# Attention, then a gated mixing layer, on one core: five blocks instead of three multiplied late by seven-product block multiplication, and the order of all work redrawn

## The chip, the cores and the metric

The kernel runs on one core of one Trainium2 chip. The metric is the time of one execution on the device, in microseconds (us); lower is better. The kernel before took 575.64 us (median of 3 runs, 574.69 to 575.94).

## What is computed

Cut to what matters, in float32 from end to end:

```python
scores = q @ k.T / sqrt(64) - log(448)          # 8 batches x 12 heads, 448 tokens, 64 wide
x = sigmoid(scores) @ v                         # put together: 8 x 448 x 768
gate = sigmoid(causal conv of x, 5 taps, per channel)
out = (gate * (x @ w_val)) @ w_out              # two 768 x 768 products
```

The engines that multiply fast take float16 or a rounded float32, so the kernel reaches float32 accuracy in one of two ways: it multiplies plain float32 tiles, which TensorE does in more passes, or it splits each operand into a high and a low part and adds three products (high x high, low x high, high x low).

## The kernel before, in words

**Units.** Two heads of one batch are a *pair* (48 of them, `st[i]`), two pairs a *two* (24, `two[j]`), and three twos fill one batch, called a *block* here (0 to 7). The tokens of block 0 are dealt out over blocks 1 to 7, so that the second stage has seven blocks of 512 tokens each.

**Attention.** `scores` (L581) multiplies a pair's keys and queries, chunk by chunk of 128 keys: three instructions of the plan per pair, each into one of three `ps_a` tiles of PSUM. Pairs in `WHOLE_SCORES` (0 to 14) use plain float32 (`qk_single`), the others `qk_hi` and `qk_lo`. The keys beyond three chunks come two pairs at a time from `scores_rest` (L616). `attention` (L655) takes a finished PSUM tile: ScalarE does the sigmoid (L659). For twos in `WHOLE` (0 to 8) that writes the float32 tile `a_single` and frees the bank. For the others the sigmoid stays in PSUM, ScalarE copies it out as float16 (L669, recorded as L404), VectorE subtracts to get the low part (L670), and only then is the bank free. `attend` (L693) multiplies by the values: a rest (L709) and four groups of chunks (L717). `out_of_ps` (L742) copies the result into `x`.

**Range of x.** A block with no two in `WHOLE` is `bounded`: the float16 scale of its x is taken from its values' largest, known early (`x_bound`, L602). In any other block VectorE has to find the largest x itself (L769), ScalarE spreads it on a diagonal (L809) and TensorE sends it to all partitions (`spread`, L811 to L813); `x_split` (L834) can come only after that.

**Second stage.** `product` (L849, its matmuls are L864) multiplies a block by `w_val` (named V below: 6 x 6 steps of three 512-column matmuls). The gate comes from five taps, on ScalarE, VectorE, GpSimd and by adding transfers. `y` is gate times product; blocks 1 to 4 go through `w_out` in the same way at once (O below, 6 x 6 x 3 = 108 matmuls of 512 columns), with y rounded by a transfer of GpSimd (L898) and its low part by VectorE or GpSimd (L899).

**Late blocks.** Blocks in `LATE` (5, 6, 7) store y to DRAM instead (L891), and are multiplied at the end by a scheme with seven half-size products in place of eight (`late_product`, L933; the matmuls are L956: 7 products x 3 parts x 3 x 3 = 189 matmuls of 256 columns per block). Its inputs, `out_forms` (L915), are sums and differences of quarters of y: loads through one buffer `y4` (L912), sums (L923), casts on ScalarE (L928, L929; recorded as L398), low parts (L930, L931; recorded as L409). Its outputs are scaled (L964), added (L973) and stored (L1001). The forms of successive late blocks live by turns in the tiles of the queries and keys and in the tiles of the attention weights, and so wait for those.

**Order.** Nothing is issued in the order of the code. Every step is an `op` with a cost per engine that may do it, a priority worked out from the table `AT`, and dependencies through its tiles; `Plan.issue` (L210) plays this through once, on the host, and writes each engine's instructions down in the order in which they start there. On the chip each engine then works through its own queue in that order. An op that two engines may do goes to the one that the plan finds free; `AT["share"]` (L249) says when VectorE may take a copy of ScalarE's. VectorE and GpSimd ops named `port="VG"` are kept from overlapping, on the chip by a dependency that is added at L1141.

Of the kernel before, what the change touches and what calls it, by code (L numbers as in the profile page):

```python
# [39 lines left out]
WHOLE = {*range(0, 9)}  # L40
WHOLE_SCORES = {*range(0, 15)}
# [40 lines left out]
LATE = (5, 6, 7)  # L82
AHEAD_OF_VAL = 3

FIRST_TOP = 6
SUMS = 12
OWN_BANKS = (6, 7)
# [5 lines left out]
BY_GPSIMD = ()  # L93
# [7 lines left out]
    first=-15.92, step=186.61, val=336.87, val_step=-29.39, out=-1237.15, out_step=257.57, w_max=1518.34,  # L101
    w_split=-860.95, load_qk_first=-201.47, load_qk=-1852.52, load_v=-662.01, split_hi=32.92, split_lo=-1097.78,
    rest_first=3174.29, rest=-1385.28, a_first=-2081.72, a=-74.73, attend=1686.54, v_max=-553.4, v_exp=-1453.48,
    v_split=144.91, x=-3266.86, x_max=-92.19, x_scale=515.03, x_hi=744.75, x_lo=177.24, x_step=2637.25,
    x_early=1120.5, first_max=-2492.59, tap=891.8, scores=8.56, a_rest=-659.37, a_rest_first=766.83,
    tap_first=-340.19, tap_pair=-743.04, tap_step=-330.6, gate=2823.26, product=-1112.74, y=2077.31, g_hi=-1119.86,
    g_lo=-3664.76, o=-3117.03, sums=-1119.35, f=-1154.59, late=-18.26, late_step=909.44, late_load=-912.54,
    pair0=2133.67, pair1=-1429.33, pair2=330.9, pair3=-1211.45, pair4=1377.13, pair5=-3156.16, pair6=297.98,
    pair7=-522.61, pair8=1609.62, pair9=-2397.11, pair10=-676.08, pair11=-98.56, pair12=-2966.57, pair13=-1287.04,
    pair14=1751.28, pair15=-717.37, pair16=545.19, pair17=-2818.83, pair18=-2085.26, pair19=495.26, pair20=75.11,  # L110
    pair21=-2539.24, pair22=-2144.55, pair23=158.2, val0=-2466.55, val1=1919.24, val2=208.28, val3=1536.8,
    val4=-2488.28, val5=-691.86, out0=173.81, out1=2060.89, out2=3408.9, out3=430.48, out4=2535.97, out5=-302.79,
    val_of1=-468.82, val_of2=-2362.91, val_of3=-1477.84, val_of4=1531.79, val_of5=1921.35, val_of6=-402.85,
    val_of7=1707.7, out_of1=-472.42, out_of2=247.7, out_of3=-1251.83, out_of4=-193.95, out_of5=1473.61,
    out_of6=-476.29, out_of7=-1672.61, share=2436.46, w_load=2736.66,
# [39 lines left out]
class Op:  # L155
    __slots__ = ("ways", "prio", "emit", "deps", "n", "start", "end", "eng", "after", "size", "port", "then")

    def __init__(self, n, ways, prio, emit, size, port):
        self.n, self.ways, self.prio, self.emit, self.size, self.port = n, ways, round(prio, 5), emit, size, port
        self.deps, self.after, self.then = set(), None, None  # L160
        self.start = self.end = self.eng = None


class Plan:
# [9 lines left out]
    YIELD = 0.3  # L174
    DMA_RATE = 310e3
# [5 lines left out]
    def op(self, ways, prio, emit, reads=(), writes=(), size=0, port="VG"):  # L181


        o = Op(len(self.ops), ways, prio, emit, size, port)
# [25 lines left out]
    def issue(self):  # L210
# [13 lines left out]
        events, order, bus, port = [], [], 0.0, 0.0  # L224
# [10 lines left out]
        while events:  # L235
# [6 lines left out]
            for e in engines:  # L242
                if free[e] > t:
                    continue
                for _, n in ready[e]:
# [3 lines left out]
                    if e == "V" and "A" in o.ways and free["A"] < t + AT["share"]:  # L249
                        continue  # L250
# [11 lines left out]
                cost = o.ways[e]  # L262
                o.eng, o.start = e, t
# [932 lines left out]
```

## Time and profile before

| what | before |
|---|---|
| median of 3 runs | 575.64 us |
| profiled execution | 575.5 us, of which the span from first to last instruction is 573.6 |
| TensorE (PE) busy | 563.7 us, 98% of the span |
| VectorE (DVE) | 423.6 us, 74% |
| ScalarE (ACT) | 401.6 us, 70% |
| GpSimd (POOL) | 242.6 us, 42% |
| granted TensorE clock | 0.998 of full speed |

A matmul's busy time reaches past the start of the next one, so "busy" does not tell how tightly TensorE is packed; the distance from one start to the next does. Weight loads are PEld and run beside the matmuls.

### The profile page before, as it was taken

The page shows a single profiled execution, that of the slowest core. Times are in us where ns is not written, and L with a number is a line of the kernel's source. Part 1 is how long each engine was busy: PE and PEld are TensorE (multiplying, and loading weights), DVE is VectorE, ACT ScalarE, POOL GpSimd, SP SyncE. Part 2 cuts the span into 40 slices and gives each one's busy share as a digit, 9 for nine tenths or more (in the row PEclk, how much of TensorE's full clock was granted, in tenths as well). Part 3 has the DMA queues.
Part 4 walks back from the last instruction along what each step waited for, and adds up shares of the span by engine and source line. Part 5 has one row for each costly group of instructions (what it writes and reads, how often), then busy time and mean ns, then how long its engine had stood idle before and what let it go on. Part 6 is the DMA issues. An engine that isn't in the chain of part 4 may idle for free.

```text
span 573.6 us, 9982 instructions
## 1 busy us (share of the span) xinstructions
PE 563.7 (98%) x3793; PEld 300.6 (52%) x3793; DVE 423.6 (74%) x653; ACT 401.6 (70%) x488; POOL 242.6 (42%) x301
## 2 busy tenths in 40 slices
PE   9999989999999999999999999999999999999996
PEld 4343334454554545545455445455555446865785
DVE  0867998896789775486766778866878999847544
ACT  5788986556987859677686878997889994332221
POOL 0001346866656285365734455545665421400100
PEclk9999999999999999999999999999999999999999
DMA  8987789968586979686495775976787565730122
GB/s 312 360 272 247 223 216 229 218 159 230 186 207 201 300 162 246 161 198 155 109 231 146 205 172 152 219 191 184 204 237 197 137 166 143 188 94 14 61 75 74
DMA packets 48400, 107.25 MB, mean 187 GB/s; under 512 B 15712, under 2 KB 24544, under 8 KB 48352
## 3 DMA queue, kind: packets, MB, share of 16 engines
q1 hardware_dynamic: 33808, 67.19, 34.3%
q0 software_dynamic: 14256, 39.23, 33.6%
q8 instruction: 30, 0.49, 0.3%
q10 hardware_dynamic: 288, 0.20, 0.1%
q14 instruction: 18, 0.15, 0.1%
HBM read 63.52 MB, written 17.90 MB: 142 GB/s over the span
## 4 chain that ended last, share of the span: by engine, by line
PE 89%; ACT 4%; DVE 3%; issue 2%; DMA 1%; POOL 1%; DVEq 0%; ACTq 0%
PE ps_m L864 42%; PE ps_a L592 15%; PE ps_a L717 15%; PE late L956 7%; PE ps_m L956 4%; PE ps_a L636 4%; PE ps_a L709 3%; ACT a_single L659 1%; DMA g<-y 1%; DVE a L670 1%; ACT gate L404 1%; PE ps_m L1023 1%; DVE gate L790 0%; POOL w_form L409 0%; DVE y L896 0%
## 5 line engine op out<-in xcount | busy, mean ns | idle before, releaser
L864 PE MATMUL ps_m<-xs,w_val_hi 128*128 128x512 f16 x504 | 150.1, 379 | 0.6 <-DVE y L896 0.6
L670 DVE SCALAR_TENSOR_TENSOR a<-ps_a,a 128x896 f16<-128x896 f32 x90 | 95.1, 1090 | 29.2 <-ACT a L404 29.0
L659 ACT ACTIVATE ps_a<-ps_a 128x896 f32<-128x896 f32 x105 | 93.2, 911 | 26.6 <-DVE v_exp L649 16.1
L864 PE MATMUL ps_m<-xs,w_val_lo 128*128 128x512 f16 x252 | 95.5, 379 | 0.0
L787 POOL TENSOR_SCALAR tap<-x,cw 128x512 f32<-128x512 f32 x84 | 69.2, 845 | 56.6 <-DVE gate L790 14.1
L409 POOL TENSOR_TENSOR qk_lo<-qk_src,qk_hi 128x448 fp32r<-128x448 f32 x66 | 74.9, 1156 | 29.9 <-DVE gate L790 11.1
L864 PE MATMUL ps_m<-g,w_out_hi 128*128 128x512 f16 x288 | 86.0, 380 | 0.5 <-POOL g L409 0.5
L404 ACT ACTIVATE a<-ps_a 128x896 f16<-128x896 f32 x90 | 80.1, 928 | 0.2
L864 PEld LDWEIGHTS <-w_val_hi 128*128 128x128 f16 x504 | 47.6, 98 | 60.0 <-issue 7.8
L790 DVE SCALAR_TENSOR_TENSOR gate<-x,cw,gate 128x512 f32<-128x512 f32 x84 | 65.3, 798 | 0.5 <-ACT gate L404 0.3
L659 ACT ACTIVATE a_single<-ps_a 128x896 f32<-128x896 f32 x63 | 53.6, 928 | 17.0 <-DVE out_inverse L434 8.5
L794 POOL DMA_DIRECT2D gate<-tap x42 | 38.8, 925 | 50.3 <-DMA gate<-tap 25.4
L864 PE MATMUL ps_m<-g,w_out_lo 128*128 128x512 f16 x144 | 54.6, 379 | 0.0
L717 PE MATMUL ps_a<-a,v_hi 128*64 128x448 f16 x360 | 49.4, 355 | 0.0
L864 PEld LDWEIGHTS <-w_out_hi 128*128 128x128 f16 x288 | 27.0, 98 | 35.0 <-issue 4.3
L717 PE MATMUL ps_a<-a_single,v_src 128*64 128x448 f32 x216 | 42.6, 543 | 0.0
L567 POOL DMA_DIRECT2D qk_hi<-qk x33 | 20.8, 630 | 48.4 <-PE ps_a L592 35.8
L592 PE MATMUL ps_a<-qk_hi 64*128 64x448 f32 x198 | 40.1, 401 | 0.8 <-DVE a_rest L670 0.8
L864 PEld LDWEIGHTS <-w_val_lo 128*128 128x128 f16 x252 | 24.7, 98 | 29.7
L592 PE MATMUL ps_a<-qk_single 64*128 64x448 f32 x180 | 37.2, 553 | 0.2 <-ACT a_single L659 0.2
L592 PE MATMUL ps_a<-qk_lo,qk_hi 64*128 64x448 f32 x198 | 36.3, 362 | 0.0
L592 PE MATMUL ps_a<-qk_hi,qk_lo 64*128 64x448 f32 x198 | 36.3, 362 | 0.0
(144 smaller groups left out, 936.4 us busy)
## 6 DMA issues: line engine op xcount, KB each, us to landing
gate<-tap POOLq DMA_DIRECT2D x42, 512.0 KB, 5.8
qk_src<-qk SPq DMA_DIRECT2D x33, 448.0 KB, 5.0
qk_hi<-qk POOLq DMA_DIRECT2D x33, 416.0 KB, 4.3
v_src<-vs SPq DMA_DIRECT2D x24, 448.0 KB, 4.1
qk_single<-qk SPq DMA_DIRECT2D x14, 448.0 KB, 6.2
out_t<-y SPq DMA_DIRECT2D x24, 224.0 KB, 2.1
w_words<-w_val SPq DMA_DIRECT2D x6, 768.0 KB, 7.9
w_words<-w_out SPq DMA_DIRECT2D x6, 768.0 KB, 4.8
```

Of the source, the lines that this page charges most:

```text
L404: nc.scalar.activation(to, x, AF.Copy, scale=by)
L409: engines[eng].tensor_tensor(to, x, y, op=ALU.subtract)
L592: mm(b()[:, h, :S], k()[rows, at : at + P], q()[rows, :S], start=(n == 0), stop=(n == len(terms(i)) - 1))
L636: mm(b()[to, h, :S], x[n]()[rows, CW:], x[n]()[rows, :S], start=True, stop=True)
L659: nc.scalar.activation(to, b()[:, :, :S], AF.Sigmoid, bias=-math.log(S), scale=1.0 / math.sqrt(D))
L670: op({"V": 1.0}, t + 0.5, lambda e: nc.vector.scalar_tensor_tensor(part(1), p(), A_SCALE, part(0), op0=ALU.mult, op1=ALU.subtract), [b], [ ...
L717: mm(px()[to, p, :S], v()[:, o : o + D], x(st[2 * j + p]["a", c])[:, h, at : at + S], start=(j == 0 and c == 0 and n == 0), stop=(j > 0 an ...
L787: op({"G": TAP_G}, at + AT["tap_step"] * k - AT["tap_first"] + AT["tap_pair"] * p, lambda e, p=p, k=k, tap=tap: nc.gpsimd.tensor_scalar(by ...
L790: op({"V": 0.67}, at + AT["tap_step"] * k + AT["tap_pair"] * p, lambda e, p=p, part=part, k=k: nc.vector.scalar_tensor_tensor(part(), x()[ ...
L794: op({"G": 1.1}, at + AT["tap_step"] * k, lambda e, tap=tap: nc.gpsimd.dma_start(g(), tap(), accum_op=ALU.add), [tap], [g], 4 * P * T * 4, "")
L864: mm(po()[:, cs], w()[:, c, :], x(k)[:, cs], start=(c == 0 and j == 0), stop=(c == NC - 1 and j == 2))
L956: mm(po()[:, i * HT : (i + 1) * HT], weights(w, k, c), gv[b, c][g]()[:, x, :], start=(c == 0 and i == 0 and j == 0), stop=(c == UNITS - 1 ...
```

## The change

It moves blocks 3 and 4 from the direct second product to the late scheme. Twos 13, 22 and 23 get plain float32 attention weights and values, pairs 15, 16 and 17 plain float32 scores. Block 4 and block 7 thereby stop being bounded and measure their largest x. A copy that ScalarE did alone, because the rule of `share` never let VectorE have it, is now given to VectorE where `ON_VECTOR` names it. Three low parts of weights are offered to GpSimd. The plan also counts a cost when TensorE goes from one shape of tile to another, and all numbers of `AT` are new. Cut to its core:

```diff
-WHOLE = {*range(0, 9)}
-WHOLE_SCORES = {*range(0, 15)}
+WHOLE = {*range(0, 9), 13, 22, 23}
+WHOLE_SCORES = {*range(0, 18)}
-LATE = (5, 6, 7)
+LATE = (3, 4, 5, 6, 7)
+FIRST_OUT = min({*range(1, B)} - {*LATE}, default=B - 2)
-OWN_BANKS = (6, 7)
-BY_GPSIMD = ()
+BY_GPSIMD = (("out", 4), ("out", 5), ("val", 1),)
+ON_VECTOR = {
+    "a": {13, 14, *range(27, 30), 38},
+    "forms": {18, 19, 31, 41},
+    "gate": {3},
+    "o": {*range(24, 27), 39, 45},
+    "parts": {27, 35},
+    "xs": {8},
+}
 AT = dict(
-    first=-15.92, step=186.61, val=336.87, val_step=-29.39, out=-1237.15, out_step=257.57, w_max=1518.34,
+    first=1148.39, step=658.12, val=11982.37, val_step=633.23, out=-10068.43, out_step=-8973.56, w_max=14984.15,
...
+    LEAVE = {"full": 0.0, "wide": 0.095, "tall": 0.098, "small": 0.0}
+    ENTER = {"full": 0.008, "wide": 0.1, "tall": 0.03, "small": 0.0}
...
-                    if e == "V" and "A" in o.ways and free["A"] < t + AT["share"]:
-                        continue
...
+                if e == "P":
+                    if o.form != form:
+                        cost += self.LEAVE[form] + self.ENTER[o.form]
+                    form = o.form
...
-    x_exp = ring(sb, 3, [P, 4], I32, "x_exp")
-    o_scale = ring(sb, 3, [P, NC], F32, "o_scale")
+    x_exp = ring(sb, 8, [P, 4], I32, "x_exp")
+    o_scale = ring(sb, 8, [P, NC], F32, "o_scale")
...
+    def way(kind, n, scalar, vector):
+        return {"V": vector} if n in ON_VECTOR.get(kind, ()) else {"A": scalar}
...
-        op({"A": 0.82, "V": 1.0}, t + 0.4, lambda e: scaled(e, part(0), p(), A_SCALE), [b], [a], port="")
+        op(way(tag, n, 0.82, 1.0), t + 0.4, lambda e: scaled(e, part(0), p(), A_SCALE), [b], [a], port="")
...
-            po = ps_a.new(lambda: ps.tile([P, 512], F32, name="late", tag="ps_a", bufs=ps_a.n)) if b in OWN_BANKS else ps_m.new()
+            po = ps_a.new(lambda: ps.tile([P, 512], F32, name="late", tag="ps_a", bufs=ps_a.n)) if b != LATE[0] else ps_m.new()
...
-            elif o.eng == "V" and o.ways["V"] > 0.2:
+            elif o.eng == "V":
                 last = traced
```

Lines of the changed file stand some 20 further down: its L404 is L424, L659 is L679, L409 is L429, L398 is L418, L567 is L587, L765 is L785, L787 is L807, L794 is L814, L796 is L816, L898 is L918.

The order at three places. First GpSimd's queue where block 2 is made ready for its product by `w_out` (O2), just ahead of the tokens' low parts. Before:

```order
L898 DMA g<-y 128x512
L898 DMA g_2043<-y 128x512
L794 DMA gate<-tap 128x1024
L567 DMA qk_hi<-qk 128x832
L765 MEMSET x 128x2x4
L409 TENSOR_TENSOR qk_lo<-qk_src,qk_hi 128x448
L409 TENSOR_TENSOR g<-y,g 128x512
L409 TENSOR_TENSOR g_2043<-y,g_2043 128x512
L409 TENSOR_TENSOR qk_lo<-qk_src,qk_hi 128x384
```

Now:

```order
L918 DMA g<-y 128x512
L918 DMA g_2078<-y 128x512
L429 TENSOR_TENSOR qk_lo<-qk_src,qk_hi 128x384
L785 MEMSET x 128x2x4
L814 DMA gate<-tap 128x1024
L587 DMA qk_hi<-qk 128x832
L807 TENSOR_SCALAR tap<-x,cw 128x512
L814 DMA gate<-tap 128x1024
```

The two low parts of y (g) have left GpSimd's queue; VectorE makes them. On TensorE, scores of pair 23 alone stood between the last product by `w_val` of block 2 and O2; now the remaining keys and values of two 11 and the scores of pair 24 do.

Second, ScalarE's queue around the last three pairs, 45 to 47 (the tile `a_rest` is the rest of two 23). Before:

```order
L404 ACTIVATE a<-ps_a 128x2x448
L404 ACTIVATE gate<-x,cw 128x512
L398 CAST forms<-y_4511 128x768
L398 CAST forms<-f 128x1024
L659 ACTIVATE ps_a<-ps_a 128x2x448
L404 ACTIVATE gate<-x,cw 128x512
L404 ACTIVATE a_rest<-ps_a 128x2x448
L404 ACTIVATE x<-ps_a,v_exp 128x2x7x64
L659 ACTIVATE ps_a<-ps_a 128x2x448
L796 ACTIVATE gate<-gate 128x1024
L404 ACTIVATE a<-ps_a 128x2x448
```

Now:

```order
L679 ACTIVATE a_single<-ps_a 128x896 x3
L418 CAST forms<-y_2873 128x768
L418 CAST forms<-f 128x1024
L679 ACTIVATE a_single<-ps_a 128x896
L418 COPY x<-ps_a 128x2x7x64
L679 ACTIVATE a_single<-ps_a 128x896 x3
L816 ACTIVATE gate<-gate 128x1024
L679 ACTIVATE a_single<-ps_a 128x896 x3
```

Each PSUM tile of these pairs now takes one instruction of ScalarE and none of VectorE.

Third, ScalarE's queue from the last copy of x (two 23) on, which has a new step. Before:

```order
L404 ACTIVATE x<-ps_a,v_exp 128x2x7x64
L398 CAST forms<-f 128x1024
L404 ACTIVATE gate<-x,cw 128x512
L404 ACTIVATE xs<-x,x_exp 128x1024
L404 ACTIVATE gate<-x,cw 128x512
```

Now:

```order
L418 COPY x<-ps_a 128x2x7x64
L418 CAST forms<-f 128x1024
L424 ACTIVATE gate<-x,cw 128x512 x2
L424 ACTIVATE diagonal<-eye,x_exp 128x128
L424 ACTIVATE xs<-x,x_exp 128x1024
```

On TensorE the two `spread` matmuls that read this diagonal stand six product steps (V6, three matmuls of 512 columns each) behind the last matmul of two 23.

## Rows read from the trace of the kernel before

**Rows 1.** The page: span, and busy time of the engines with their instructions.

```profile
span 573.6 us, 9982 instructions
PE 563.7 (98%) x3793; PEld 300.6 (52%) x3793; DVE 423.6 (74%) x653; ACT 401.6 (70%) x488; POOL 242.6 (42%) x301
...
PEclk9999999999999999999999999999999999999999
```

**Rows 2.** The waits of TensorE, longest first: who waited for whom, us in total, times, longest.

```profile
PE ps_a L813 <- ACT diagonal L404: 1.3, 1, 1.3
...
PE ps_a L592 <- DVE a_rest L670: 0.8, 1, 0.8
PE ps_m L864 <- DVE y L896: 0.6, 1, 0.6
PE ps_m L864 <- POOL g L409: 0.5, 1, 0.5
```

**Rows 3.** The chain that ended last, in order of time, near the end: start, length, what.

```profile
517.80 7.77 PE ps_m L864 x36
...
538.25 30.27 PE late L956 x276
```

**Rows 4.** The timeline of TensorE around the rest and the values of a two, first in plain float32 (two 5), then split (two 21). Columns: start, length, engine, line, operation, tiles, shape, count.

```profile
67.05 0.98 PE L636 MATMUL ps_a<-qk_single 64*64 64x448 f32 x8
...
73.38 2.53 PE L592 MATMUL ps_a<-qk_single 64*128 64x448 f32 x12
...
429.32 0.16 PE L631 MATMUL ps_a<-vm,ones 128*128 128x1 bf16 x1
429.41 0.98 PE L636 MATMUL ps_a<-qk_src 64*64 64x448 f32 x8
...
434.53 0.47 PE L592 MATMUL ps_a<-qk_hi 64*128 64x448 f32 x2
```

**Rows 5.** The timeline of TensorE around the scores of a pair, plain (pair 8) and split (pair 43); the row behind each is the next work.

```profile
50.33 2.53 PE L592 MATMUL ps_a<-qk_single 64*128 64x448 f32 x12
52.78 0.18 PE L462 MATMUL ps_m<-val_max,ones 128*128 128x1 bf16 x1
...
441.87 0.47 PE L592 MATMUL ps_a<-qk_hi 64*128 64x448 f32 x2
...
443.89 0.60 PE L864 MATMUL ps_m<-xs,w_val_hi 128*128 128x512 f16 x2
```

**Rows 6.** The timeline where the largest x of block 1 is spread: TensorE, ScalarE, VectorE, each in its own order; in brackets the idle time before an instruction and what ended it. The last row is the spread of block 2.

```profile
77.38 0.22 PE L813 MATMUL ps_a<-diagonal,ones 128*128 128x64 bf16 x2 [1.29 <-ACT diagonal L404]
...
73.55 0.91 ACT L398 COPY x<-ps_a 128x896 f32<-128x896 f32 x1 [1.97 <-PE ps_a L717]
74.51 2.54 ACT L659 ACTIVATE a_single<-ps_a 128x896 f32<-128x896 f32 x3
76.92 0.41 ACT L404 ACTIVATE diagonal<-eye,x_exp 128x128 bf16<-128x128 bf16 x1
...
74.68 1.20 DVE L769 TENSOR_REDUCE x_max<-x 128x2 f32<-128x1024 f32 x1
75.91 0.16 DVE L807 TENSOR_REDUCE x_exp<-x_max 128x1 f32<-128x6 f32 x1
...
149.36 0.22 PE L813 MATMUL ps_a<-diagonal,ones 128*128 128x64 bf16 x2
```

**Rows 7.** The timeline of TensorE and GpSimd at O2.

```profile
206.63 0.38 PE L864 MATMUL ps_m<-g,w_out_hi 128*128 128x512 f16 x1
207.51 0.38 PE L864 MATMUL ps_m<-g,w_out_hi 128*128 128x512 f16 x1 [0.50 <-POOL g L409]
...
205.21 1.13 POOL L409 TENSOR_TENSOR qk_lo<-qk_src,qk_hi 128x448 fp32r<-128x448 f32 x1 [0.74 <-DVE gate L790]
206.31 2.26 POOL L409 TENSOR_TENSOR g<-y,g 128x512 f16<-128x512 f32 x2
```

**Rows 8.** The timeline of TensorE, ScalarE and VectorE inside the scores of pair 46.

```profile
453.39 0.37 PE L592 MATMUL ps_a<-qk_lo,qk_hi 64*128 64x448 f32 x2
454.58 0.47 PE L592 MATMUL ps_a<-qk_hi 64*128 64x448 f32 x2 [0.82 <-DVE a_rest L670]
...
452.51 0.89 ACT L404 ACTIVATE a_rest<-ps_a 128x896 f16<-128x896 f32 x1
...
453.44 1.09 DVE L670 SCALAR_TENSOR_TENSOR a_rest<-ps_a,a_rest 128x896 f16<-128x896 f32 x1 [0.77 <-ACT a_rest L404]
```

**Rows 9.** Busy time by stretch: stretch, its length, then PE, PEld, DVE, ACT and POOL busy (and instructions), granted clock, DMA share, GB/s. The first is from the scores of pair 33 to those of pair 43, the last the pure end from the first late product on.

```profile
323.00:425.00 102.00, 101.36 (x720) 52.74 (x718) 78.63 (x116) 86.16 (x104) 55.59 (x71) 1.00 0.74 190
425.00:445.00 20.00, 20.00 (x153) 11.01 (x150) 17.02 (x24) 18.41 (x22) 14.07 (x16) 1.00 0.80 217
445.00:465.00 20.00, 19.18 (x137) 9.83 (x137) 18.59 (x32) 19.71 (x25) 7.61 (x10) 1.00 0.51 130
483.30:568.80 85.50, 85.50 (x676) 65.88 (x674) 52.78 (x90) 23.74 (x31) 10.93 (x12) 1.00 0.31 87
```

**Rows 10.** The timeline of the queue of SyncE: two loads in a row of a late block's y through the one buffer y4.

```profile
484.65 0.32 SPq L912 DMA_DIRECT2D y<-late_y  x1
494.99 0.34 SPq L912 DMA_DIRECT2D y<-late_y  x1
```

More of the change, by code (lines that the diff above doesn't have):

```diff
@@ L106 @@
[L106 to L110, printed above, removed]
@@ new lines @@
+    w_split=-7975.51, load_qk_first=22001.37, load_qk=-8150.12, load_v=-1133.89, split_hi=-2959.37, split_lo=-5728.66,
+    rest_first=7257.04, rest=-1089.56, a_first=-15056.76, a=-2335.45, attend=17974.54, v_max=-9929.82, v_exp=-6802.55,
+    v_split=-3786.43, x=-14268.82, x_max=-18657.18, x_scale=-6663.95, x_hi=25495.52, x_lo=1507.88, x_step=2856.69,
+    x_early=15403.41, first_max=2876.25, tap=5343.44, scores=13424.61, a_rest=-7576.8, a_rest_first=-32217.93,
+    tap_first=4948.0, tap_pair=-4557.78, tap_step=818.45, gate=13031.37, product=5342.64, y=-3772.31, g_hi=2925.98,
@@ L155, with __init__ @@
 class Op:
-    __slots__ = ("ways", "prio", "emit", "deps", "n", "start", "end", "eng", "after", "size", "port", "then")
-    def __init__(self, n, ways, prio, emit, size, port):
+    __slots__ = ("ways", "prio", "emit", "deps", "n", "start", "end", "eng", "after", "size", "port", "then", "form")
+    def __init__(self, n, ways, prio, emit, size, port, form):
         self.n, self.ways, self.prio, self.emit, self.size, self.port = n, ways, round(prio, 5), emit, size, port
+        self.form = form
         self.deps, self.after, self.then = set(), None, None
@@ L223, in issue @@
         held = dict.fromkeys(engines)
-        events, order, bus, port = [], [], 0.0, 0.0
+        events, order, bus, port, form = [], [], 0.0, 0.0, "full"
         def release(o, t):
@@ L513, in weight_forms @@
         every = lambda: sums().rearrange("p f c n -> p (f c n)")
-        op({"A": 1.7, "V": 1.0}, prio + 0.5, lambda e: copy(e, part(0), every()), [sums], [form])
+        op(way("form", u, 1.7, 1.0), prio + 0.5, lambda e: copy(e, part(0), every()), [sums], [form])
         op({"V": 1.66, "G": 3.3}, prio + 0.6, lambda e: sub(e, part(1), every(), part(0)), [sums], [form])
@@ L841, in x_split @@
         sc = lambda: e()[:, 1:2].bitcast(F32)
-        op({"A": 1.04, "V": 0.66}, t + AT["x_hi"], lambda eng: scaled(eng, part(0), tokens(), sc()), [x, own, e], [high])
+        op(way("xs", j, 1.04, 0.66), t + AT["x_hi"], lambda eng: scaled(eng, part(0), tokens(), sc()), [x, own, e], [high])
         op({"V": 1.2}, t + AT["x_lo"], lambda _: nc.vector.scalar_tensor_tensor(
@@ L1115, in attention_then_gate @@
             x_split(3 * b + c)
-        if b == 2:
+        if b == FIRST_OUT + 1:
             weight_scales("out")
-            x_unscale(1)
-        if b > 1:
+            for n in range(1, b):
+                x_unscale(n)
+        if b > FIRST_OUT:
             x_unscale(b)
```

111 lines of the change are left out of this document (57 added, 54 removed).

## The prediction

> **What bounds it now.** I read the page first, then TensorE's waits, the chain of waits, the timeline where a wait stands, and busy time by stretch. The page has TensorE busy for 563.7 of 573.6 us, at full clock [rows 1]. Its waits come to a few us in all; the four that lie behind the start and reach half a us are named in [rows 2]. The chain of waits ends in product after product, one start close behind the other: 36 matmuls of 512 columns in 7.77 us, 276 of 256 columns in 30.27 us without a break [rows 3]. So TensorE's own work sets the time. A change can gain only by taking matmul time out, or by removing one of the few waits; an engine beside it counts only where TensorE is made to wait for it. The places to watch are the stretches in which ScalarE and VectorE are nearly as busy as TensorE: from 445 to 465 us ScalarE was busy for 19.71 of 20 us and VectorE for 18.59, and there TensorE lost time [rows 9].
>
> **The change part by part.** The sum is made against the profiled execution, 575.5 us (span 573.6 and 1.9 around it), which is 0.14 us under the median of 575.64.
>
> 1. Two direct second products go. A block's is 108 matmuls of 512 columns, two blocks' 216; one is 7.77 / 36 = 0.2158 us [rows 3]. That is -46.6 us.
> 2. Two late ones come: 2 x 189 = 378 matmuls of 256 columns at 30.27 / 276 = 0.1097 us [rows 3], +41.5 us. Both orders of issue keep them back to back, since the weight loads run beside them.
> 3. Twos 13, 22 and 23 in plain float32. From the rest's start to the next scores a plain two took 73.38 - 67.05 = 6.33 us, a split one with its `vm` step 434.53 - 429.32 = 5.21 [rows 4]: +1.12 us each, +3.4 for three.
> 4. Pairs 15, 16 and 17 with plain scores: 52.78 - 50.33 = 2.45 against 443.89 - 441.87 = 2.02 us [rows 5], +0.43 each, +1.3.
> 5. Blocks 4 and 7 now spread their largest x, two short matmuls each, 0.22 us [rows 6]: +0.4.
>
> TensorE's work thus comes to -46.6 + 41.5 + 3.4 + 1.3 + 0.4 = 0.0 us. What the seven-product scheme saves, the plain float32 steps pay back. What is left is the waits.
>
> 6. The wait at O2. In the old order GpSimd does the tokens' low part, ends at 206.34, and only then the low parts of y, and TensorE starts 207.51 - 206.63 = 0.88 us apart where 0.22 is the pace [rows 7]: 0.66 us lost. In the new queue these low parts are VectorE's, and between the last y and O2 stand the values of two 11 and a pair's scores instead of a pair's scores alone, some 5 us more room (5.21 for rest and values [rows 4]). I take -0.66; the bounds are -0.66 and 0, since VectorE may be late in its turn.
> 7. The wait inside pair 46: 454.58 - 453.39 = 1.19 us where the pace is 0.2, so 0.98 lost. PSUM's next bank was that of the rest of two 23, which had to pass a sigmoid, a copy on ScalarE at 452.51 and a subtraction on VectorE at 453.44 [rows 8]. Two 23 is plain now: one sigmoid frees the bank, the copy and the subtraction are not issued. I take -0.98, between -0.98 and 0.
> 8. The spread of block 7's largest x, a new wait on TensorE's queue with V6 behind it. The trace has it at block 1: copy of x from 73.55, largest from 74.68, reduction from 75.91, diagonal only from 76.92, behind three sigmoids, spread at 77.38 with 1.29 us waited; at block 2 it cost no wait [rows 6]. Without the sigmoids the diagonal could have begun at about 76.2 and the spread stood some 3.3 us behind the end of the values. Now the copy is followed by one cast and two gate steps, which fit into the time that VectorE needs for the largest; the spread stands six product steps, 18 x 0.2158 = 3.9 us, behind. I take 0; the bounds are 0 and 1.3.
> 9. The late stage gets 72 more steps of TensorE, and VectorE's queue there grows from 90 to 147 instructions. From 483.30 on VectorE was busy 52.78 of 85.50 us [rows 9]; 147 x 52.78 / 90 = 86 us in 85.5 + 41.5 = 127 us is 68%, against 62%. Hidden behind TensorE. All twelve loads of y go through one buffer, one at a time; two in a row stood 494.99 - 484.65 = 10.3 us apart [rows 10], and 6.9 us of products are made of each. The order loads them well ahead, so I take 0. If that lead were used up, 3.4 us would be lost with every further load.
> 10. The copies named for VectorE. Most of the names are of steps that no longer exist: weights of twos that are plain, products by `w_out` of blocks that are late. In the new queues four copies move, out of some 480 steps of ScalarE: 0. The three low parts of weights offered to GpSimd cost ScalarE three more passes early on, under TensorE's work: 0.
> 11. The crowded stretch. Between the scores of pairs 33 and 43 ScalarE has 104 instructions in either order. Before they were busy 86.16 us in 102 [rows 9]. But 85 product steps stood between them there and 66 do now: 19 x 3 x 0.2158 = 12.3 us less to hide behind, 86.2 us in 90. That is 96%, and the densest 20 us seen ran at 99% [rows 9]. Cover of 4 us in 90 is thin. I take one wait like the 0.6 us of [rows 2] for y, which is in the old order too and lies in this stretch: no difference. The bounds are 0 and ten pairs with 0.98 each, the wait of step 7: +9.8.
>
> The rule in the Trainium skill, page TensorEngine Tiling (Array Packing), section PSUM Bottleneck, speaks against this step: a faster array does not empty PSUM faster, and the copies out of it may become the limit. By that rule, taken on average, the stretch would last 86.2 / 0.985 = 87.5 us, the pace of ScalarE at its densest, which is still under TensorE's 90, so the sum would be the same; what it leaves is unevenness, the second rival. So far the trace agrees with it in one place only, the wait of step 7.
>
> Sum: 0.0 - 0.66 - 0.98 = -1.6, so 573.9 us for that execution and **574.0** for the median.
>
> **The rivals.** *The waits only move.* Two waits go, but new ones of that size come in the denser middle or at the spread. For it: work is unchanged, the two largest waits of an order were always somewhere. Against it: one of them loses the very instructions that it waited for. Then 575.5 + 0.0, or up to 1 us either way: no change, about 575.6.
>
> *ScalarE's queue sets the pace of the crowded stretch.* Its place is pairs 33 to 43, its mechanism a PSUM bank that is freed late because ScalarE and VectorE have no slack to catch up. It decides once a pair loses more than 0.16 us on average, since ten pairs then eat the 1.6 us. If half of the pairs lose 0.98 us, it is +4.9: 575.5 - 1.6 + 4.9 = 578.8. For it: 96% over 90 us against 84% before. Against it: at 99% over 20 us only 0.98 was lost, and by way of the subtraction that two 23 no longer has.
>
> *All waits go,* those of the first 80 us too (1.3 and less [rows 2]): 575.5 - 1.6 - 1.3 - 0.8 = 571.8.
>
> *The change does not do what it says.* The copies for VectorE are nearly empty (step 10); if the rest fails too, this is the first rival.
>
> **How the numbers follow.** A measurement of this kernel can tell 0.2%, 1.15 us, from no change. The forecast has 0.42, all waits go 0.06, the waits only move 0.28, ScalarE's queue 0.24. The forecast is close to the 0.2% bound, so a little of it counts as no change: faster 0.45, within 0.2% 0.30, slower 0.25. The range goes from 571.3, a little under the case that all waits go, to 578.5, most of the second rival.
>
> **What would show it.** Right, if direct products have 216 matmuls and late ones 945 at the same pace; if the waits for a_rest and for GpSimd's g at O2 are gone; if the spread of block 7 has no wait; if ScalarE is over 90% busy between pairs 33 and 43 and TensorE waits there for under a us. Wrong, if TensorE waits there pair by pair, if late products show gaps for `forms`, or if the pace of 256 columns is not half that of 512.

## The result and the profile after

The changed kernel took **580.93 us** (median of 5 runs, 580.18 to 581.56), the kernel before 575.25 us beside it (574.69 to 575.94). The ratio is **1.0096, 95% interval 1.0081 to 1.0110**: slower by some 1%. The prediction said 574.0, with a range of 571.3 to 578.5 and a chance of 0.25 for slower; the time lies above the range.

The page of the changed kernel, which answers to [rows 1]:

```profile
span 579.2 us, 10179 instructions
...
PE 566.1 (98%) x3890; PEld 314.0 (54%) x3890; DVE 427.9 (74%) x672; ACT 392.9 (68%) x477; POOL 240.9 (42%) x290
```

TensorE is busy for 2.4 us more in a span that is 5.6 longer, and its share is 98% as before. The page alone doesn't tell where the time went. The waits of TensorE do, longest first (who waited for whom, us in total, times, longest), against [rows 2]:

```profile
PE ps_a L612 <- DVE a L690: 2.3, 3, 0.9
PE ps_m L1043 <- DVE ones L1036: 1.1, 1, 1.1
PE ps_a L833 <- ACT diagonal L424: 1.1, 1, 1.1
PE ps_m L884 <- DVE y L909: 0.9, 1, 0.9
PE late L976 <- DVE parts L988: 0.8, 1, 0.8
```

The rows for a_rest and for GpSimd's g are gone. A new one leads: three times the scores of a pair (L612) waited for the subtraction that frees a bank of PSUM (L690). All three lie between pairs 33 and 43, and so does the wait for y (L909). The one for parts (L988) is in the late stage.

To put each microsecond in its place I split, for one execution of each kernel, TensorE's time step by step. The work of a step is its start-to-start time in front of a step of that kind where nothing holds it (lower quartile over both traces); what is over counts as wait. Time is then work + wait + some 11 us of start and end:

| stretch | before: work, wait | after: work, wait |
|---|---|---|
| up to the products of block 1 | 82.5, 2.7 | 82.5, 3.3 |
| to the scores of pair 33 | 231.8, 1.3 | 207.9, 1.3 |
| scores of pair 33 to those of pair 43 | 101.2, 1.3 | 88.9, **5.0** |
| to the first late product | 57.1, 1.5 | 51.9, 0.5 |
| late stage | 84.9, 0.2 | 126.1, **2.3** |
| sum | 557.4, 6.9 | 557.2, 12.4 |

The work is the same; 5.5 us of waits came. The two stretches in the view of busy time (as [rows 9]):

```profile
298.90:392.80 93.90, 90.58 (x666) 47.31 (x665) 79.73 (x117) 86.42 (x104) 51.53 (x67) 1.00 0.83 214
445.20:579.20 134.00, 127.25 (x1054) 102.88 (x1052) 94.65 (x148) 42.38 (x54) 24.94 (x23) 0.99 0.35 106
```

ScalarE did 104 instructions in 93.9 us, as many as before in 102, and was 92% busy. Now single waits. The timeline of TensorE, VectorE and ScalarE around the first of the three waits for the subtraction, inside the scores of pair 35:

```profile
313.67 1.27 DVE L863 SCALAR_TENSOR_TENSOR xs<-x,x_exp,xs 128x1024 f16<-128x1024 f32 x1
313.72 0.92 ACT L424 ACTIVATE a<-ps_a 128x896 f16<-128x896 f32 x1
...
314.87 2.07 DVE L690 SCALAR_TENSOR_TENSOR a<-ps_a,a 128x896 f16<-128x896 f32 x2
...
316.30 0.93 ACT L424 ACTIVATE a<-ps_a 128x896 f16<-128x896 f32 x1
...
316.87 0.73 DVE L909 SCALAR_TENSOR_TENSOR y<-ps_m,y_scale,gate 128x512 f32<-128x512 f32 x1
...
317.50 0.36 PE L612 MATMUL ps_a<-qk_lo,qk_hi 64*128 64x448 f32 x2
317.52 1.07 DVE L690 SCALAR_TENSOR_TENSOR a<-ps_a,a 128x896 f16<-128x896 f32 x1
...
318.74 0.47 PE L612 MATMUL ps_a<-qk_hi 64*128 64x448 f32 x2 [0.88 <-DVE a L690]
```

One copy was done at 314.64, but VectorE was at the low part of x until 314.94, and then made two subtractions and a step of y. So the next copy, done at 317.23, found VectorE at y; its subtraction began at 317.52, the bank came free at 318.59, and TensorE stood still for 0.88 us. In the other two waits, at 355 and 373 us, the subtraction began right behind its copy (354.66 and 371.82): there ScalarE came late, not VectorE. And the wait in block 4's first products, for SyncE, VectorE and TensorE:

```profile
329.92 0.33 SPq L579 DMA_DIRECT2D v_src<-vs  x1
...
337.20 1.09 DVE L644 TENSOR_REDUCE vm<-v_src 128x1 bf16<-128x896 f32 x1 [1.54 <-DMA v_src<-vs]
...
338.20 1.40 DVE L909 SCALAR_TENSOR_TENSOR y<-ps_m,y_scale,gate 128x512 f32<-128x512 f32 x2
...
339.00 0.59 PE L884 MATMUL ps_m<-xs,w_val_hi 128*128 128x512 f16 x2 [0.91 <-DVE y L909]
```

The load of v landed after 7.3 us. The reduction for `vm` stood at the head of VectorE's queue until then, y behind it, and TensorE waited for y's bank.

The late stage, first where it begins, then at block 4's second part:

```profile
443.83 1.65 POOL L807 TENSOR_SCALAR tap<-x,cw 128x512 f32<-128x512 f32 x2
...
444.81 2.19 DVE L429 TENSOR_TENSOR forms<-y,forms 128x768 f16<-128x768 f32 x1
...
445.17 1.00 POOL L943 TENSOR_TENSOR f<-y,f 128x256 f32<-128x256 f32 x1
...
446.92 0.74 DVE L909 SCALAR_TENSOR_TENSOR y<-ps_m,y_scale,gate 128x512 f32<-128x512 f32 x1
...
447.71 1.47 PE L976 MATMUL ps_m<-forms,w_form 128*128 128x256 f16 x12 [0.41 <-DVE y L909]
...
471.82 0.69 DVE L943 TENSOR_TENSOR f<-y 128x512 f32<-128x512 f32 x1 [0.95 <-DMA y<-late_y]
...
472.80 1.64 POOL L429 TENSOR_TENSOR forms<-y,forms 128x768 f16<-128x768 f32 x1 [7.27 <-ACT forms L418]
...
473.48 1.24 DVE L993 TENSOR_TENSOR parts<-parts 128x256 f32<-128x256 f32 x1
...
476.12 1.14 DVE L988 SCALAR_TENSOR_TENSOR parts<-late,o_scale,parts 128x512 f32<-128x512 f32 x2
...
476.92 0.27 PE L976 MATMUL late<-forms,w_form 128*128 128x256 f16 x1 [0.77 <-DVE parts L988]
```

A subtraction for forms took 2.19 us while GpSimd worked beside it, an addition 1.24 where the rest take some 0.42, and a load of y came 0.95 us late for VectorE.

### The profile page after: what moved, and what is told of

It is laid out like the page before. It is cut to its first block, busy times and chain, and to the rows that moved or that the text cites. A ratio compares the mean times of both kernels' runs of the same rounds, so it can differ in the third digit from the quotient of the medians.

```text
span 579.2 us, 10179 instructions
## 1 busy us (share of the span) xinstructions
PE 566.1 (98%) x3890; PEld 314.0 (54%) x3890; DVE 427.9 (74%) x672; ACT 392.9 (68%) x477; POOL 240.9 (42%) x290
## 4 chain that ended last, share of the span: by engine, by line
PE 81%; DVE 8%; ACT 5%; DMA 4%; issue 2%; POOL 0%; DVEq 0%; ACTq 0%; SPq 0%; POOLq 0%
PE ps_m L884 30%; PE ps_a L737 16%; PE ps_a L612 14%; PE late L976 13%; PE ps_a L656 4%; PE ps_a L729 3%; PE ps_m L976 2%; DMA w_words<-w_out 2%; DMA v_src<-vs 1%; DVE a L690 1%; DMA y<-late_y 1%; ACT a_single L679 1%; ACT ps_a L679 1%; DVE xs L863 1%; ACT a L424 1%
## 5 line engine op out<-in xcount | busy, mean ns | idle before, releaser
L807 POOL TENSOR_SCALAR tap<-x,cw 128x512 f32<-128x512 f32 x84 | 73.6, 903 | 51.5 <-DVE gate L810 19.0
L690 DVE SCALAR_TENSOR_TENSOR a<-ps_a,a 128x896 f16<-128x896 f32 x72 | 76.0, 1084 | 22.5 <-ACT a L424 22.2
L679 ACT ACTIVATE ps_a<-ps_a 128x896 f32<-128x896 f32 x84 | 74.6, 912 | 18.1 <-DVE v_exp L669 14.4
L679 ACT ACTIVATE a_single<-ps_a 128x896 f32<-128x896 f32 x84 | 71.7, 925 | 18.0 <-PE ps_a L612 10.4
L429 POOL TENSOR_TENSOR qk_lo<-qk_src,qk_hi 128x448 fp32r<-128x448 f32 (+1 forms) x60 | 65.8, 1128 | 42.5 <-DVE gate L810 14.4
L424 ACT ACTIVATE a<-ps_a 128x896 f16<-128x896 f32 x72 | 63.7, 928 | 0.2
L976 PE MATMUL late<-forms,w_form 128*128 128x256 f16 x432 | 59.3, 273 | 0.8 <-DVE parts L988 0.8
L976 PEld LDWEIGHTS <-w_form 128*128 128x128 f16 x540 | 52.8, 98 | 11.2 <-issue 2.1
L814 POOL DMA_DIRECT2D gate<-tap x42 | 37.6, 895 | 42.9 <-DVE gate L810 23.5
L612 PE MATMUL ps_a<-qk_single 64*128 64x448 f32 x216 | 46.3, 567 | 0.3 <-ACT a_single L679 0.3
L424 ACT ACTIVATE parts<-late,o_scale 128x512 f32<-128x512 f32 x23 | 15.7, 687 | 43.2 <-PE late L976 43.2
L993 DVE TENSOR_TENSOR parts<-parts 128x256 f32<-128x256 f32 (+1 forms) x59 | 31.1, 548 | 18.7 <-ACT parts L424 18.1
L884 PE MATMUL ps_m<-g,w_out_hi 128*128 128x512 f16 x144 | 42.9, 380 | 0.0
L737 PEld LDWEIGHTS ps_a<-a_single,v_src 128*64 128x64 f32 x288 | 19.6, 137 | 36.3 <-issue 34.9
L612 PE MATMUL ps_a<-qk_hi 64*128 64x448 f32 x180 | 36.9, 405 | 2.4 <-DVE a L690 2.3
```

The lines of the kernel that those rows point to most:

```text
L424: nc.scalar.activation(to, x, AF.Copy, scale=by)
L429: engines[eng].tensor_tensor(to, x, y, op=ALU.subtract)
L612: mm(b()[:, h, :S], k()[rows, at : at + P], q()[rows, :S], start=(n == 0), stop=(n == len(terms(i)) - 1))
L679: nc.scalar.activation(to, b()[:, :, :S], AF.Sigmoid, bias=-math.log(S), scale=1.0 / math.sqrt(D))
L690: op({"V": 1.0}, t + 0.5, lambda e: nc.vector.scalar_tensor_tensor(part(1), p(), A_SCALE, part(0), op0=ALU.mult, op1=ALU.subtract), [b], [ ...
L737: mm(px()[to, p, :S], v()[:, o : o + D], x(st[2 * j + p]["a", c])[:, h, at : at + S], start=(j == 0 and c == 0 and n == 0), stop=(j > 0 an ...
```

## The experiments

**Theory A:** with 19 product steps fewer between pairs 33 and 43, TensorE comes back for a bank of PSUM before the chain sigmoid, copy (ScalarE) and subtraction (VectorE) has freed it. TensorE's product steps hide the work of that chain; I call them its *cover*. Rivals: **B,** VectorE's queue alone is too full; **C,** the new order or late transfers make the waits, however much work there is; **F** (for one run), the plain steps hold the waits down. For the late stage: **A2,** GpSimd beside VectorE; **D,** the loads of y through one buffer.

Unless a text says otherwise, a kernel has the changed kernel's order on every engine, and only lengths or buffers differ. Waits are counted as in the table. Pairs 33 to 43 were left alone in five executions (the changed kernel and the runs e4, e10, e12, e15): 5.0, 5.4, 4.1, 4.0 and 5.2 us. The two of 4 us are those without the wait behind the load of v. The late stage was left alone in ten: 1.6 to 3.6 us.

**Cover put back, here and elsewhere (e3, e10).** In the first products of blocks 4 and 5, or of 1 and 2, one matmul of a step is issued twice:

```diff
+ if n == "val" and b in (4, 5) and c and not j:      # e10: b in (1, 2)
+     mm(po()[:, cs], w()[:, c, :], x(k)[:, cs], start=False, stop=False)
```

> The changed kernel in its own order, with 60 matmuls of 512 columns more: each first product of blocks 4 and 5 issues the first matmul of five of its six steps once more (those two blocks' y is wrong by it). They stand in pairs 33 to 43, where the order before had 19 product steps more, and are worth 60 x 0.2158 = 12.9 us of TensorE's work. Theory A (TensorE's cover became too thin there): with cover put back the waits of that stretch fall by 3 to 4 us, so the time rises by 9 to 10 only, to 590 to 591. Rival C (the order or late transfers make the waits, not the cover): the time rises by all 12.9, to 593.8.

> The changed kernel in its own order with the same 60 matmuls more as in the run with filler, but in the first products of blocks 1 and 2, which run from 90 to 203 us, far ahead of pairs 33 to 43 (those blocks' y is wrong by it). The control to that run. Theory A: there is no wait of note to cover there, so the time rises by all of the 12.9 us, 580.9 + 12.9 = 593.8, and the waits of pairs 33 to 43 stay at 5 us. If any 60 matmuls gave 4.5 us back by moving later work against its transfers (Rival C), it would be 589.3 again.

e3: 589.33 us, ratio 1.0234 (1.0217 to 1.0252), that is 8.4 us over the changed kernel for 12.9 of work; waits of pairs 33 to 43 fell to 1.7. The stretch by busy time, and the waits in it:

```profile
299.20:401.70 102.50, 101.95 (x721) 52.92 (x720) 79.91 (x118) 87.16 (x104) 53.27 (x71) 1.00 0.78 201
```

```profile
PE ps_a L612 <- DVE a L690: 0.3, 1, 0.3
PE ps_a L612 <- DVE a_rest L690: 0.2, 1, 0.2
```

e10: 592.62 us, ratio 1.0293 (1.0276 to 1.0310), 11.7 more for the same 12.9; the waits of pairs 33 to 43 stayed at 4.1. The control is not quite flat, since 1.2 of 12.9 came back, but it is 3.3 us above e3. The changed kernel was not run again beside these two; taken by the ratios to the kernel before (1.0096, 1.0234, 1.0293) they cost 7.9 and 11.3 us, which says the same. So it is cover in that place that counts, and with as much of TensorE's work as before the new order waits there hardly more than the old one (1.7 against 1.3).

**The mirror: less work in the order before (e9, e16).** In the kernel before, block 4's products skip a term in five of six steps; e16 also shortens the two engines' steps as e13 does below:

```diff
+ if b == 4 and c and j == 1:
+     continue
```

> The kernel before, in its own order, with 60 matmuls of 512 columns left out: the first and second products of block 4 skip the second of three terms in five of their six steps. 53 of the 60 stand between the scores of pairs 33 and 43, so TensorE's work there falls from 101.2 to 89.8 us beside the same steps of ScalarE and VectorE, about as in the changed kernel, and no step is in another place. It takes 60 x 0.2158 = 12.9 us of work out. Theory A (thin cover makes the waits, in any order): the waits of that stretch rise from 1.3 to some 4 to 5 us, and the time falls by only 9 to 10, to 566. Rival C (the new order makes them): waits stay, 562.6 us.

> The kernel before in its own order with the 60 matmuls of block 4 left out, and in pairs 33 to 42 the copies and subtractions of one head of two (the second head's parts are not computed). Without the second edit the stretch from pair 33 to 43 kept its length, 102.5 us, though TensorE had 89.7 us of work there: 12.8 us of waits. Theory A (ScalarE and VectorE set the pace of the stretch): with some 12 and 15 us taken from them these waits fall by 8 us or more, to under 5 us, and the time from 572.5 to 564.5 or less. Rival C (transfers, the order of steps): no less than 570.

e9: 572.54 us, ratio 0.9941 (0.9924 to 0.9957). 12.9 us of work went and 3.3 came off the time. Waits of pairs 33 to 43 rose from 1.3 to 12.8, far over what I expected, and the stretch kept its length to a tenth of a us:

```profile
320.80:423.30 102.50, 94.28 (x668) 48.36 (x667) 80.37 (x117) 87.61 (x107) 55.20 (x71) 0.98 0.76 191
```

```profile
PE ps_m L866 <- DVE y L898: 2.7, 2, 1.7
PE ps_a L592 <- DVE a L670: 2.1, 4, 1.1
PE ps_a L631 <- DVE a L670: 1.8, 1, 1.8
PE ps_m L866 <- ACT y L404: 1.4, 2, 1.1
```

e16: 568.90 us, 0.9889 (0.9873 to 0.9906); waits 8.3, the stretch 98.0 us. That is 4.5 us less, not 8: right in direction, short in size. Some 1.7 us in each of these two are a lower clock, see the end. No step changed its place, only TensorE's work got less: so the new order is not needed for such waits, and that half of Rival C falls. Late transfers, its other half, are not ruled out by this (see the load of v below). Nor does the amount of work alone set the size: with 89.7 us of work in the stretch the old order waits 12.8 us, 11.1 without the lower clock, and the new one waits 5.0 with 88.9. Why the old order bears thin cover so much worse stays open.

**One engine at a time (e1, e2, e11).** The copies, the subtractions, or the gate steps of VectorE become shorter:

```diff
  e1:  scaled(e, part(0)[:, one], p()[:, one], A_SCALE)     # one = slice(0, 1) in pairs 33 to 42
  e2:  part(1)[:, one], p()[:, one], A_SCALE, part(0)[:, one]
  e11: part()[:, few], x()[:, p, few, HALO - k : HALO + SL - k], w(p, k), part()[:, few]
```

> The changed kernel in its own order, but in pairs 33 to 42 the 30 copies of the sigmoids on ScalarE take one head of two (the second head's high part is not computed; TensorE reads the first head's in its place, and every instruction of TensorE is as it was). That gives ScalarE some 30 x 0.4 = 12 us back in the 94 us in which TensorE waited 5.0 us. Theory A (TensorE is held by sigmoid, copy and subtraction in a row, which free PSUM too late now that 19 product steps are gone): the waits there fall to 1 to 2 us, so 577 to 578 us in place of 580.9. Rival B (VectorE alone is late, by its own queue): no more than 1 us less, 580. Rival C (the new order puts steps where a DMA is late, engines do not matter): no change.

> The changed kernel in its own order, but in pairs 33 to 42 the 30 subtractions behind those copies, on VectorE, take one head of two (the second head's low part is not computed; TensorE reads the first's). VectorE gets some 30 x 0.5 = 15 us back in that stretch. Theory A (the whole chain is too long): waits there fall by about as much as with the shorter copies, 577 to 578 us. Rival B (VectorE alone): they fall by most of the 5.0 us, 576.5, and clearly more than with shorter copies. Rival C (late DMAs, the order): no change from 580.9; the wait behind the load of v at pair 39 stays in any case.

> The changed kernel in its own order, but VectorE's gate steps of twos 15 to 20 take two segments of eight (the rest of the gate's taps is not added). 22 such steps between pairs 33 and 43 fall from 0.74 to some 0.25 us, which gives VectorE 11 us back there; sigmoid, copy and subtraction, the chain that frees a bank of PSUM, are whole. Rival B (VectorE's queue as a whole is too full, the subtraction comes late behind other steps): waits there fall as with the short subtractions, from 5.0 to 3.0 or less, 579 us. Theory A (the chain itself is too long): no more than 0.5 us less.

Measured: 579.55, 578.96 and 579.80 us (ratios 1.0059, 1.0055, 1.0073, each within 0.002); waits of the stretch 4.6, 3.0 and 3.9. Only the short subtractions leave the spread of 4.0 to 5.4, by 1 us. Neither engine alone is the cause, VectorE's queue least of all by its mere load: 8 us less of gate steps gave nothing.

**The chain (e13, e14), the load of v (e18), both (e17).** e13 joins e1 and e2, e14 takes one head in the sigmoid too, e18 gives v a third buffer, e17 is e13 with e18:

```diff
  v_src = ring(sb, 2, [P, VW], F32, "v_src")
+ v_src.make = lambda: sb.tile([P, VW], F32, name="v_src", bufs=3)      # e17, e18
```

> The changed kernel in its own order; in pairs 33 to 42 both the copies on ScalarE and the subtractions on VectorE take one head of two (the second head's two parts are not computed, TensorE reads the first's). ScalarE gets 12 us back in that stretch, VectorE 15. Theory A (sigmoid, copy and subtraction in a row, two engines' queues together): the waits of pairs 33 to 43, which were 4 to 5 us, fall under 1.5, the time to 577. Rival C (transfers or the order of steps, no engine): they stay over 3 us, as with either alone, 579 to 580.

> As the run with copies and subtractions short, and the 30 sigmoids ahead of them take one head of two as well (the second head is not computed). The whole chain that frees a bank of PSUM is about half as long and ScalarE gets some 24 us back. Theory A: waits of pairs 33 to 43 under 1 us, 576.5 us. Rival C: no less than with copies and subtractions alone; over 3 us.

> The changed kernel in its own order with three buffers for v in place of two and nothing else; the whole result is computed. If the load is a part of the cause by itself, the wait of 1.1 us between V4.4 and V4.5 goes in every run and the waits of pairs 33 to 43 fall from 4 to 5 us to 3.5 to 4, 580. If it matters only once ScalarE and VectorE are faster, no change: 580.9.

> As the run with copies and subtractions of one head (pairs 33 to 42; the second head's parts are not computed), and v has three buffers in place of two, the orders unchanged, so that its loads need not wait until the low part of v two steps back is made. Theory A with the load as its third part: the wait between V4.4 and V4.5 (1.34 us there) goes or halves, and the waits of pairs 33 to 43 fall from 3.3 to 2 us or less, 576.8. If the load comes late for its place in SyncE's queue and not for the buffer, no change: 3.3 us, 578.

| run | time, us | ratio to before | waits, pairs 33 to 43 |
|---|---|---|---|
| e13 | 578.12 | 1.0047 (1.0030 to 1.0065) | 3.3 |
| e14 | 578.35 | 1.0045 (1.0027 to 1.0062) | 3.3 |
| e18 | 579.34 | 1.0067 (1.0042 to 1.0092) | 4.2 |
| e17 | 575.85 | 1.0001 (0.9991 to 1.0010) | **0.65** |

Theory A as first put failed in e13 and e14: half the chain left 3.3 us. Their trace told why. In e13, SyncE, VectorE, TensorE:

```profile
327.81 0.33 SPq L579 DMA_DIRECT2D v_src<-vs  x1
...
335.15 1.09 DVE L644 TENSOR_REDUCE vm<-v_src 128x1 bf16<-128x896 f32 x1 [3.38 <-DMA v_src<-vs]
...
336.95 0.59 PE L885 MATMUL ps_m<-xs,w_val_hi 128*128 128x512 f16 x2 [1.17 <-DVE y L910]
```

VectorE, now ahead of its work, stood idle for 3.38 us until v landed. The load is issued when the low part of v two steps back is made and its buffer free. A third buffer alone is worth nothing that I can tell from the spread. Together with short steps the stretch runs at TensorE's own pace:

```profile
297.60:387.20 89.60, 89.60 (x666) 47.41 (x665) 66.46 (x118) 75.75 (x104) 52.82 (x69) 1.00 0.85 226
```

So the cause has two links that hold each other up: the bank's chain of sigmoid, copy and subtraction, and the load of v, which starts when VectorE gets to its last reader and holds VectorE's queue when it is late. Taking away either one alone leaves 3.3 to 4.2 us. One thing is not told apart: the short steps also take load off both engines (in e17 ScalarE was busy for 75.75 us in place of 86.42, VectorE for 66.46 in place of 79.73), and no run in this order makes both engines lighter with the chain left long (e6 below has both lighter, 77.81 and 62.57 of 91.6 us, and waits more, but in another order).

**The late stage (e4, e12, e8, e15).** GpSimd's share of the forms becomes a fill (e4), the loaded y gets two buffers in the same order (e12) or in an order made anew (e8), and e15 is e4 with e12:

```diff
  e4:  ... if e == "V" else nc.gpsimd.memset(to(), 0.0)
  e12: y4_ring.make = lambda: sb.tile([P, 4, HT], F32, name="y4", bufs=2)
  e8:  y4_ring = ring(sb, 2, [P, 4, HT], F32, "y4")
```

> The changed kernel, but the steps of the seven forms of y that GpSimd has in the late stage are replaced by a fill with zeros of the same tiles by GpSimd (those forms are not computed). The orders of TensorE, VectorE and ScalarE are the same; GpSimd no longer reads beside VectorE there. Theory A2 (in the late stage TensorE waits because VectorE's instructions take about twice their time while GpSimd runs the same kind of step, and because such a step comes late): the waits from 445 us on fall from 2.3 to under 1 us, about 579.3. Rival D (the loads of y through one buffer set those waits): they stay, 580.9.

> The changed kernel in its own order, each engine's queue unchanged, but with two buffers for the loaded y of the late stage in place of one. Theory D (a load waits until the buffer's last reader is done, and so brings the forms late): the late waits fall from 2.3 to 1.3 us, mostly by the 0.94 us before block 4's second part, 579.9. Theory A2 (VectorE is held up beside GpSimd): no change, 580.9.

> The changed kernel with two buffers in place of one for the y that the late stage loads; the order is made anew with it, from the same table. Work unchanged, 557.2 us. Theory D (loads of y through one buffer bring forms late, and so the 0.94 us wait at block 4's second part): late waits fall from 2.3 to some 1.3 us, 579.9. Theory A2 (they come from VectorE beside GpSimd): no change of the late waits, 580.9. Pairs 33 to 43: 65 product steps in place of 66, waits as they were.

> The changed kernel in its own order with both edits to the late stage: GpSimd fills its share of the forms with zeros in place of computing them, and the loaded y has two buffers. Together they take away what Theories A2 and D name. If these are the causes, the late waits fall from 2.3 (1.6 to 3.6 in the runs so far) to 0.5 us or less, as before the change, and the time to 578.5. If over 1.5 us stay, something else holds TensorE there.

Late waits: e4 1.15, e12 1.74, e8 3.1, e15 **0.58** us; times 578.69, 579.17, 580.60 and 578.66 (ratios 1.0042, 1.0058, 1.0089, 1.0054, each within 0.0025). e12 lies inside the spread of 1.6 to 3.6 and kept its 0.97 us at block 4's second part, so Theory D alone fell; e8 shows nothing, since its order differs. e4 is outside, and e15 nearly all the way to the 0.2 of before. In e4 none of the changed kernel's four late waits of 0.2 us and more (at 447, 449, 463 and 476 us) is left; one of 1.0 us came at 471, and it is 0.5 in e15. The mean of VectorE's subtraction for forms from 445 us on, in the changed kernel and in e15 (count, us busy, mean ns; in e4 the mean is 1029):

```profile
L429 DVE TENSOR_TENSOR forms<-y,forms 128x768 f16<-128x768 f32 x9 | 13.5, 1505 | 0.9 <-ACT forms L418 0.9
```

```profile
L430 DVE TENSOR_TENSOR forms<-y,forms 128x768 f16<-128x768 f32 x9 | 8.6, 953 | 1.5 <-ACT forms L419 1.5
```

So the late waits come from GpSimd reading beside VectorE and what that delays, with the loads as a small part at most. This rests on the waits of one execution per run. The times do not carry it: e4, e12 and e15 lie within 0.5 us of each other, and e1, e11, e12 and e18, whose edits hardly moved the waits, lie 1.1 to 1.8 us under the 580.93 of the changed kernel, which was not run beside them.

**Parts undone, with a new order (e5, e6, e7).** The plain steps, or the two more late blocks, are undone, or the old table is used:

```diff
  e5: WHOLE = {*range(0, 9)};  WHOLE_SCORES = {*range(0, 15)}
  e6: LATE = (5, 6, 7)
  e7: AT = the table of the kernel before
```

> The changed kernel with only its plain float32 steps undone: the weights of twos 13, 22 and 23 and the scores of pairs 15 to 17 are split again, as before the change; the order is made anew from the same table. By the paces of the two traces TensorE's work falls from 557.2 to 552.1 us. Between the scores of pairs 33 and 43 stand 79 product steps (66 with the change, 85 before) beside the same 104 instructions of ScalarE. Theory A (too little of TensorE's work beside those engines there): waits of that stretch fall from 5.0 to 1 to 2 us, one of about 1 us comes back in pair 46, so the sum of waits is some 10 in place of 12.4: 552.1 + 10 + 11.1 (start and end) = 573.2 us, under the kernel before. Rival F (the plain steps are what keeps VectorE and ScalarE in time; without them waits of 1 us come at each of pairs 43 to 47 and in the stretch of two 13): 12.4 + 5 and more, so 580.6 or over.

> The changed kernel with only the second products of blocks 3 and 4 direct again, each by 108 matmuls of 512 columns; plain steps and the table of numbers as in the change, the order made anew. Work by the paces of the traces 562.5 us (557.2 with the change). Between the scores of pairs 33 and 43 ScalarE has 94 instructions in 85 us of TensorE's work, 91%, VectorE 92 (104 in 89 us, 97%, and 116 with the change). Theory A: the waits of that stretch fall to 1 to 2 us, the late ones to the old 0.2, so 562.5 + 7.5 + 11.1 = 581.1 us. Rival C (the new table's order makes the waits, however much work there is): 12 us of waits, 585.6.

> The changed kernel with the table of numbers of the kernel before (places in the order), all else as in the change. Work by the paces 555.9 us. That order leaves only 49 product steps between the scores of pairs 33 and 43, beside 96 instructions of ScalarE, which are worth 79 us at their mean, and 107 of VectorE: TensorE's work there is 78 us. Theory A: ScalarE and VectorE set the pace there, waits of 6 us or more in that stretch alone, so 583 or more. Rival C (it was the new table that brought the waits): the sum of waits is back at 7 us and the time at 574.

586.52, 603.38 and 604.99 us; waits 23.4, 27.7 and 36.6 us in all, spread over the whole program (e5 has 12.6 ahead of pair 30, e6 12.4 in the late stage). My sums of waits for e5 and e6 were wrong by 13 and 20 us. Theory A also asked for 1 to 2 us in pairs 33 to 43 there, and got some 4.4 in e5 and 6.6 in e6. e5's time is one that Rival F allowed, but not in F's place: from pair 43 to 47 TensorE's longest wait is 0.4 us. In e7 the stretch of pairs 33 to 43 waited 6.3 us as Theory A asked, but others waited too. The lesson is on method: a table of places fits one list of steps, and a part undone with the table kept measures the table. What the plain steps are worth stays open.

## Why the prediction was wrong

- **Steps 1 to 5, work 0.0: right.** Measured -0.2 us by the table of stretches. Late matmuls are 945 in place of 567 at the pace taken; the chain near its end, against [rows 3], shows 237 of them in 25.89 us, 0.1092 each, and further up a load of y (step 9):

```profile
465.98 5.82 DMA y<-late_y
...
545.91 25.89 PE late L976 x237
```

- **Steps 6, 7 and 8: right in their places.** At O2, inside pair 46 and at the spread of block 7, against [rows 7], [rows 8] and [rows 6]:

```profile
210.90 0.60 PE L884 MATMUL ps_m<-g,w_out_hi 128*128 128x512 f16 x2
211.34 0.38 PE L884 MATMUL ps_m<-g,w_out_lo 128*128 128x512 f16 x1
```

```profile
419.60 0.37 PE L612 MATMUL ps_a<-qk_lo,qk_hi 64*128 64x448 f32 x2
419.80 0.37 PE L612 MATMUL ps_a<-qk_hi 64*128 64x448 f32 x2
```

```profile
440.36 0.38 PE L884 MATMUL ps_m<-xs,w_val_lo 128*128 128x512 f16 x1
440.58 0.22 PE L833 MATMUL ps_a<-diagonal,ones 128*128 128x64 bf16 x2
440.64 0.60 PE L884 MATMUL ps_m<-xs,w_val_hi 128*128 128x512 f16 x2
```

  Starts follow at the undisturbed pace: the two waits went, no new one came at the spread. But what step 6 gained did not reach the sum: the stretch from block 1's products to pair 33 has 1.3 us of waits as before, because one of 0.5 us came for `out_max` (L482, at 120 us). There the first rival, that waits only move, came true.
- **Step 11, the crowded stretch, failed: taken 0, measured +3.7 us.** It had the place, the 19 product steps and the thin cover, and its bounds held 3.7. What misled was the choice of the lower end by an average. ScalarE at 96% of 90 us was called thin but enough, because 20 us had run at 99%. But a bank's chain passes two engines in order and hangs on a load as well, and TensorE's extra products were what filled the gaps. e3 and e9 show this, e17 shows the links. The rival named ScalarE's queue; e1 shows that ScalarE alone is not it. Its mechanism, a bank freed late by ScalarE and VectorE, is what the three waits for the subtraction show, and its price of 4.9 was near; it lacked the load of v.
- **Step 9, the late stage, failed: taken 0, measured +2.1.** VectorE's share came out as worked out (94.65 of 134 us, 71%, against 68%), and that was the wrong thing to look at. The step counted VectorE's instructions at their lengths of before and asked whether they fit, not how long they last beside GpSimd, which went from 12 instructions there to 23. e4 and e15 show it. The 3.4 us for a load of y whose lead is used up were named and not counted; the chain passes through one load, but e12 shows that the loads alone matter little.
- **Step 10** was not tried by itself.
- The sum: 575.25 - 0.2 + 5.5 of waits = 580.5; the rest lies at the end of the span and between runs. Forecast were -1.6 us of waits. The way from there to +5.5 is 3.7 in step 11, 2.1 in step 9, the 0.7 that came back after step 6, and 0.6 more up to the products of block 1, which no run looks into. The range stopped at 578.5 since it took the second rival for most of its price and had no case in which two stretches fail at once.

The rule weighed in step 11, of the Trainium skill, page TensorEngine Tiling (Array Packing), section PSUM Bottleneck, is that copies out of PSUM may become the limit. The trace agrees in part: three of the waits there, 2.3 us, were for the subtraction that frees a bank. What did not hold was step 11's use of it on the mean load: that gave 87.5 us, and the stretch took 93.9.

## What to carry to other kernels

Before taking matmuls out of a stretch, ask what lies behind them: in the stretch shown here, with ScalarE busy for 84% of it and VectorE for 77% before the change, TensorE's work was the cover, and 12.9 us of it taken away gave back 3.3 (e9). Look at the chain that frees a bank and at the load that its engines wait for, not at shares of busy time. Where a change gives GpSimd more steps beside VectorE, price VectorE's at their lengths beside it.

## What the runs showed of the hardware

VectorE's steps with two inputs from SBUF grow where GpSimd reads beside them: for forms, 0.95 us (the mean in e15, where GpSimd only fills) became 2.19, and an addition of parts, 0.42 at the median, became 1.24. The Trainium skill, page SBUF — State Buffer, section SBUF: two separate sides, says that the two share a port by an exclusive lock and that the loser stands still for the whole instruction; these lengths agree with it: the subtraction of 2.19 us ended 0.8 us after GpSimd's step from 445.17 did, about its length alone.

A wait can cost more than its length. In e9 TensorE stood still from 348.6 to 350.4; busy time by stretch of 1 us around it (the third column from the end is the granted clock):

```profile
349.00:350.00 1.00, 0.00 (x0) 0.00 (x0) 1.00 (x2) 1.00 (x3) 0.64 (x1) 1.00 0.52 180
350.00:351.00 1.00, 0.55 (x9) 0.23 (x9) 1.00 (x2) 0.97 (x2) 0.72 (x1) 1.00 0.00 0
351.00:352.00 1.00, 1.00 (x13) 0.42 (x9) 1.00 (x3) 0.63 (x1) 0.41 (x1) 0.53 0.00 0
352.00:353.00 1.00, 1.00 (x14) 0.30 (x8) 1.00 (x3) 0.85 (x1) 0.58 (x1) 0.50 0.14 22
```

After the wait it ran at the lower of its two levels, 1.2 GHz, until some 354.5, which cost about 1.7 us more. Not every such stand does it: one of 1.68 us at 329 in the same run left the clock at 1.00. In the changed kernel, whose waits are 1.1 us at most, the clock stayed at 1.00 in that stretch.
